# Gate and up products of a GEGLU block taken two 512-token blocks at a time, one weight load for two matmuls

## The chip, the core and the metric

The kernel runs on one core of a Trainium2 chip. Its engines run side by side and meet through semaphores: PE (TensorE, matmuls), PEld (PE's weight loads, which the profile lists apart), ACT (ScalarE), DVE (VectorE), POOL (GpSimd) and SP (which here only issues DMAs). The metric is the time of one execution on the device, in microseconds; of several runs the median is given.

## What is computed

The input `x` has 2048 tokens of 640 values, in bfloat16. Two branches are mixed by a gate per token:

```
x = A_x
g = sigmoid((x * gate_w).sum(-1, keepdims=True))
a = linear_attention(x, A_wqkv, A_wo)                       # 32 heads of 20
b = (gelu(x @ B_w_gate) * (x @ B_w_up)) @ B_w_down          # 640 -> 1728 -> 640
return g * a + (1 - g) * b
```

The change concerns `x @ B_w_gate`, `x @ B_w_up`, the gelu and the product of the two.

## The kernel before

Everything lies in one SBUF tensor, `pool`, and one PSUM tensor, `ps`, of 8 banks of 128 x 512 float32. The transposed input `xT` has 5 chunks `k` of 128 model dimensions; a matmul's weights are a 128 x 128 block, its moving operand 128 x 512 (one block `j` of 512 tokens, one bank of output).

The stages in order: the q and k products and their feature maps (L453 to L558), the product of keys and x with its evacuation (L596 to L634), then the long loop over `ffn`, which this change is in, then the output stage (L811 to L876), which adds the attention part and the down product in PSUM, scales it and sends it out.

The loop at the end of the attention setup runs over g = 0 to 55: 14 blocks `fc` of hidden units by 4 token blocks `j`, `j` the inner one. `G(g)` makes one block: five matmuls of the gate weights into one bank and five of the up weights into another (L700), a gelu of the gate bank on ACT into one of three float32 buffers `ge` (L706), and a multiply of the up bank by it on DVE into `hT` (L708). The last hidden block is only 64 wide: for `fc` = 13, `G13` has gate and up weights in the two halves of one weight block, so one bank and five matmuls a call (L678), gelu at L682, multiply at L685.

Banks come from a rotation of three pairs, which G and W2 share:

```
PAIRS = [(0, 1), (2, 3), (6, 7)]
def next_pair():
    p = PAIRS[pair_ctr[0] % 3]
    pair_ctr[0] += 1
    return p
```

In the text P0, P1 and P2 are these pairs. A G of one block takes a pair and uses its first bank for gate and its second for up. Banks 4 and 5 belong to KV; G13 takes 4, 5, 6, 7 in turn.

Other work is put between the G calls by the loop: `KV(0)` after g = 5 and `KV(1)` after g = 6 (L721, mask at L727), `W2(c)` after each of g = 8 to 13 (two short matmuls at L739 and L740 into a pair, a copy on ACT at L742, DMAs through SP), and from g = 14 on `N(i)` after each even g: a product on POOL (L754), five operations on DVE (L756 to L764) and a transpose DMA through SP. After the loop the w_down loads are issued on SP, once N has freed their place.

The order on each engine is the order of the calls of `P.op(engine, fn, reads, writes)`. It works out what each operation must wait for from its reads and writes (a bank written by PE waits for those that read it last), attaches the waits to the operation's first instruction and one semaphore increment to its last. A `P.op` of ten matmuls thus tells others of its end once. Each engine then works its list off in order.

Of the kernel before, what the change touches and what calls it, by code (L numbers as in the profile page):

```python
# [6 lines left out]
ACT = mybir.ActivationFunctionType  # L7
ALU = mybir.AluOpType
# [8 lines left out]
KC = D // 128  # L17
# [145 lines left out]
def bass_gated_mix__linear_attn_block__geglu_ffn__prompt_kernel(  # L163
# [63 lines left out]
    with (  # L227
# [8 lines left out]
        with contextlib.ExitStack() as stack:  # L236
            dma_sems = [stack.enter_context(nc.semaphore("s_in%d" % i)) for i in range(n_dma_in)]

            P = _Plan(["pe", "act", "dve", "pool", "sp"])
# [9 lines left out]
            def new_dma_key():  # L249
                k = "in%d" % dma_next[0]  # L250
                dma_next[0] += 1
                return k

            def v16(o, n):
                return pool[:, o:o + n]

            def v32(o, n):
                return pool[:, o:o + 2 * n].bitcast(F32)
# [7 lines left out]
            xT = v16(R_XT, KC * S).rearrange("p (k s) -> p k s", k=KC)  # L266
# [5 lines left out]
            wg = v16(R_WG, KC * 1664).rearrange("p (k f) -> p k f", k=KC)  # L272
            wu = v16(R_WG + KC * 1664, KC * 1664).rearrange("p (k f) -> p k f", k=KC)
            wgu = v16(R_WG + 2 * KC * 1664, KC * 128).rearrange("p (k f) -> p k f", k=KC)
# [8 lines left out]
            hT = [v16(R_B + fc * S, S) for fc in range(NFC)]  # L283
# [5 lines left out]
            ge = [v32(R_E + n * 1024, 512) for n in range(3)]  # L289
# [15 lines left out]
            bank = [P.res("bank%d" % b, excl=True) for b in range(8)]  # L305
            r_xn = [P.sb("xn%d" % i, R_XN + i * XW, R_XN + (i + 1) * XW) for i in range(NT)]
            r_pk = [P.sb("pk%d" % i, R_PK + i * 640, R_PK + (i + 1) * 640) for i in range(NT)]
            r_xT = [P.sb("xT%d" % i, R_XT, R_XT + KC * S) for i in range(NT)]
# [5 lines left out]
            r_wg = P.sb("wg", R_WG, R_WG + KC * 1664)  # L314
            r_wu = P.sb("wu", R_WG + KC * 1664, R_WG + 2 * KC * 1664)
            r_wgu = P.sb("wgu", R_WG + 2 * KC * 1664, R_WG + 2 * KC * 1664 + KC * 128)
# [20 lines left out]
            r_ratio = P.res("ratio")  # L337
            r_gw = P.res("gw")

            def dma_in(dst, src, writes, reads=(), eng="sp"):  # L340
                P.op(eng, lambda e, dst=dst, src=src: e.dma_start(dst, src),  # L341
                     reads=reads, writes=writes, dma=new_dma_key())
# [3 lines left out]
            def load_x(i, eng="sp"):  # L346
                dma_in(x_aug[:, i, 0:640], A_x[0, i * 128:(i + 1) * 128, :], [r_xn[i]], eng=eng)

            def load_wk(k, eng="sp", after=()):
                dma_in(wk[:, k, :], A_wqkv[k * 128:(k + 1) * 128, 640:1280], [r_wk[k]], reads=after, eng=eng)  # L350
# [6 lines left out]
            def load_wq(k, eng="sp"):  # L357
                dma_in(wq[:, k, 0:640], A_wqkv[k * 128:(k + 1) * 128, 0:640], [r_wq[k]], eng=eng)
# [3 lines left out]
                 writes=[P.res("touch")], dma=new_dma_key())  # L362
# [25 lines left out]
            for c in range(NHC):  # L388
# [9 lines left out]
                 reads=[r_ones], writes=[r_ident])  # L398
# [167 lines left out]
            for i in range(NQ, NT):  # L566
                KQ(i)
                if i == 4:
                    late_constants()
            P.op("dve", lambda e: e.tensor_scalar(gg, eg, 0.5, 0.5, ALU.mult, ALU.add),  # L570
                 reads=r_eg, writes=[r_g])
            P.op("dve", lambda e: e.tensor_scalar(omg, eg, -0.5, 0.5, ALU.mult, ALU.add),
                 reads=r_eg, writes=[r_omg])
# [7 lines left out]
                 reads=[r_omg], writes=[r_od], dma=new_dma_key())  # L581
# [44 lines left out]
            def ME(g):  # L626
# [6 lines left out]
                for c in cs:  # L633
# [8 lines left out]
                 reads=r_pk[0:2], writes=[r_tmp[0]])  # L642
            for i in range(2, NT):
                P.op("dve", lambda e, i=i: e.tensor_tensor(zacc, zacc, pk[i], ALU.add),  # L644
                     reads=[r_tmp[0], r_pk[i]], writes=[r_tmp[0]])
# [7 lines left out]
            r_hT = [[P.sb("hT%d_%d" % (fc, j), R_B + fc * S + j * 512, R_B + fc * S + (j + 1) * 512)  # L653
                     for j in range(NSC)] for fc in range(NFC)]
            r_ge = [P.sb("ge%d" % n, R_E + n * 1024, R_E + (n + 1) * 1024) for n in range(3)]
# [5 lines left out]
# [5 lines that stand above are left out]
            ffn = [(fc, j) for fc in range(NFC) for j in range(NSC)]  # L666
            single_ctr = [0]

            def G13(g):
                fc, j = ffn[g]  # L670
                n = g % 3
                b = (4, 5, 6, 7)[single_ctr[0] % 4]
                single_ctr[0] += 1

                def fn(e):
                    last = None
                    for k in range(KC):
                        last = e.matmul(ps[:, b, :], wgu[:, k, :], xT[:, k, j * 512:(j + 1) * 512],  # L678
                                        start=(k == 0), stop=(k == KC - 1))
                    return last  # L680
                P.op("pe", fn, reads=[r_wgu] + r_xT[4 * j:4 * j + 4], writes=[bank[b]])
                P.op("act", lambda e: e.activation(ge[n][64:128, :], ps[0:64, b, :], ACT.Gelu_apprx_tanh),  # L682
                     reads=[bank[b]], writes=[r_ge[n]])
                h = j % 2
                P.op("dve", lambda e: e.tensor_tensor(  # L685
                    hT[fc][64 * h:64 * h + 64, j * 512:(j + 1) * 512], ps[64:128, b, :], ge[n][64:128, :], ALU.mult),
                    reads=[bank[b], r_ge[n]], writes=[r_hT[fc][j]])

            def G(g):
                fc, j = ffn[g]  # L690
                if fc == 13:
                    return G13(g)
                gb, ub = next_pair()
                n = g % 3

                def mk(w, b):
                    def fn(e):
                        last = None
                        for k in range(KC):
                            last = e.matmul(ps[:, b, :], w[:, k, fc * 128:(fc + 1) * 128],  # L700
                                            xT[:, k, j * 512:(j + 1) * 512], start=(k == 0), stop=(k == KC - 1))
                        return last
                    return fn
                P.op("pe", mk(wg, gb), reads=[r_wg] + r_xT[4 * j:4 * j + 4], writes=[bank[gb]])
                P.op("pe", mk(wu, ub), reads=[r_wu] + r_xT[4 * j:4 * j + 4], writes=[bank[ub]])
                P.op("act", lambda e: e.activation(ge[n], ps[:, gb, :], ACT.Gelu_apprx_tanh),  # L706
                     reads=[bank[gb]], writes=[r_ge[n]])
                P.op("dve", lambda e: e.tensor_tensor(hT[fc][:, j * 512:(j + 1) * 512], ps[:, ub, :],  # L708
                                                      ge[n], ALU.mult),
                     reads=[bank[ub], r_ge[n]], writes=[r_hT[fc][j]])  # L710

            def KV(h):
                cs, b = (((0, 1, 2, 3), 4), ((4, 5), 5))[h]

                def fn(e):
                    last = None
                    for n, c in enumerate(cs):
                        e0 = 120 * c if c < 5 else 512
                        w = 120 if c < 5 else 40
                        for k in range(KC):  # L720
                            last = e.matmul(ps[:, b, n * 120:n * 120 + w], wv[:, k, e0:e0 + 128],  # L721
                                            mT[:, k, 120 * c:120 * c + w], start=(n == 0 and k == 0),
                                            stop=(k == KC - 1), skip_group_check=True)
                    return last
                P.op("pe", fn, reads=[r_wv] + r_mT + r_mTt, writes=[bank[b]])
                lo, hi = (0, 480) if h == 0 else (480, 640)
                P.op("dve", lambda e: e.tensor_tensor(kvl[:, lo:hi], ps[:, b, 0:hi - lo], mask[:, lo:hi],  # L727
                                                      ALU.mult),
                     reads=[bank[b], r_mask], writes=[r_kvl[h]])
# [40 lines left out]

            n_done = 0
            for g in range(len(ffn)):
                G(g)
                if g in (5, 6):
                    KV(g - 5)
                if 8 <= g < 8 + NHC:
                    W2(g - 8)
                if g == 16:
                    r_ob = P.sb("omgb", R_OB, R_OB + 2 * S)
                    dma_in(omg_b, omg_dram.unsqueeze(0).broadcast_to([128, S]), [r_ob], reads=[r_od])  # L780
                if g >= 14 and g % 2 == 0 and n_done < NT:
                    N(n_done)
                    n_done += 1
# [145 lines left out]
```

## Time and profile before

| | |
|---|---|
| median of 3 runs | 273.87 us (273.70 to 273.97) |
| the profiled execution, first to last instruction (span) | 272.6 us, granted TensorE clock 1.00 |
| median less that span | 1.27 us |
| gate and up products begin / N begins / 64-wide block begins / output stage begins | 70.4 / 106.7 / 185.9 / 190.0 us |
| last matmul starts | 270.5 us |

The profiled execution's time is known by its span alone; the times of runs come from other executions. A group line of the profile reads: line, engine, operation, output <- input, shape, count | busy time in us, mean ns of one | idle time of the engine before them, and what ended it. In an answer in order of time a line reads: start and length in us, engine, line, operation, shapes, count, and in brackets the idle time before. A line of the chain that ended last reads: start, length, engine, line, count. A few per cent of the matmul records can be missing. Busy time by stage, in us:

| from : to | PE | PEld | DVE | ACT | POOL |
|---|---|---|---|---|---|
| 70.4 : 83.4 (G to KV) | 12.95 | 5.88 | 4.74 | 5.46 | 2.77 |
| 86.9 : 103.7 (G with W2) | 16.69 | 8.19 | 5.01 | 7.69 | 0.00 |
| 103.7 : 170.8 (G with N) | 66.78 | 30.43 | 62.71 | 19.20 | 19.67 |
| 170.8 : 190.2 (G, G13) | 19.30 | 8.82 | 9.52 | 5.94 | 0.00 |
| 190.2 : 272.6 (output) | 80.17 | 36.71 | 4.13 | 11.47 | 0.00 |

### The profile page before, as it was taken

What the parts mean: (1) busy time and instruction counts of PE and PEld (TensorE: products, weight loads), DVE (VectorE), ACT (ScalarE), POOL (GpSimd) and SP (SyncE); (2) the same over time, 40 slices, a digit from 0 to 9 for tenths busy, and PEclk for the clock granted to TensorE, in tenths of its full rate; (3) what the DMA queues carried; (4) which work ended last, traced back from release to release, by engine and by line L of the source; (5) the groups of instructions that cost most, each with busy time, mean ns of one, the idle gap of its engine ahead of it and who ended that gap; (6) DMA issues with size and microseconds to landing.
All of it is one profiled execution on the core that took longest, in us unless ns stands there. A gap on an engine that the chain in (4) does not pass through costs nothing.

```text
span 272.6 us, 3416 instructions
## 1 busy us (share of the span) xinstructions
PE 267.6 (98%) x1341; PEld 127.9 (47%) x1367; DVE 140.8 (52%) x247; ACT 75.9 (28%) x132; POOL 30.0 (11%) x28
## 2 busy tenths in 40 slices
PE   8999999999999999999999999999999999999997
PEld 3555555544445454444444444444444444444444
DVE  1678989997233335999999999634210000000200
ACT  2455555210422453232222233224011122121021
POOL 5000000003240002242332422000000000000000
DMA  7976999600200011514121221273031110110211
GB/s 192 202 115 127 346 399 388 140 2 19 58 19 2 23 50 51 192 34 49 26 48 25 49 48 27 60 219 105 5 77 38 41 38 19 38 41 19 58 58 41
DMA packets 42864, 23.78 MB, mean 87 GB/s; under 512 B 32223, under 2 KB 41439, under 8 KB 42719
## 3 DMA queue, kind: packets, MB, share of 16 engines
q1 hardware_dynamic: 42517, 23.22, 31.9%
q10 hardware_dynamic: 330, 0.33, 0.3%
q8 instruction: 11, 0.18, 0.3%
q14 instruction: 6, 0.05, 0.1%
HBM read 13.83 MB, written 2.63 MB: 60 GB/s over the span
## 4 chain that ended last, share of the span: by engine, by line
PE 96%; DMA 1%; SPq 1%; issue 1%; DVE 0%
PE ps L700 41%; PE ps L864 23%; PE ps L539 12%; PE ps L596 6%; PE ps L843 4%; PE ps L468 2%; PE ps L811 2%; PE ps L678 2%; PE ps L599 1%; DMA pool<-in_A_x_dram 1%; PE ps L453 1%; PE ps L824 1%; SPq L341 1%; PE ps L721 1%; SPq L353 0%
## 5 line engine op out<-in xcount | busy, mean ns | idle before, releaser
L700 PE MATMUL ps<-pool 128*128 128x512 bf16 x510 | 113.0, 379 | 0.5
L700 PEld LDWEIGHTS ps<-pool 128*128 128x128 bf16 x520 | 50.5, 98 | 60.0
L864 PE MATMUL ps<-pool 128*128 128x512 bf16 (+2 forms) x300 | 62.4, 366 | 0.3
L706 ACT ACTIVATE pool<-ps 128x512 f32<-128x512 f32 x52 | 31.0, 597 | 73.1 <-PE ps L700 73.1
L708 DVE TENSOR_TENSOR pool<-ps,pool 128x512 bf16<-128x512 f32 x52 | 34.7, 689 | 31.7 <-PE ps L700 30.4
L864 PEld LDWEIGHTS ps<-pool 128*128 128x128 bf16 x306 | 29.2, 98 | 33.4 <-issue 0.4
L847 DVE TENSOR_TENSOR pool<-ps,pool 128x512 bf16<-128x512 f32 x4 | 2.8, 690 | 61.5 <-PE ps L843 61.5
L539 PE MATMUL ps<-pool 128*128 128x512 bf16 (+1 forms) x176 | 32.5, 343 | 0.2
L754 POOL TENSOR_TENSOR pool<-pool 128x640 f32<-128x640 bf16 x16 | 22.4, 1404 | 73.0 <-DVE pool L756 65.6
L871 ACT ACTIVATE pool<-ps,pool 128x512 bf16<-128x512 f32 (+1 forms) x16 | 10.9, 680 | 68.6 <-PE ps L864 68.6
L539 PEld LDWEIGHTS ps<-pool 128*128 128x128 bf16 x180 | 17.6, 98 | 15.0
L558 DVE SCALAR_TENSOR_TENSOR pool<-ps,pool 128x128 bf16<-128x128 f32 (+2 forms) x36 | 21.7, 602 | 2.1
L549 ACT ACTIVATE pool<-ps 128x640 bf16<-128x640 f32 x24 | 16.9, 703 | 15.8 <-DVE pool L558 9.3
L596 PE MATMUL ps<-pool 128*128 128x512 bf16 x76 | 19.2, 379 | 0.1
L764 DVE TENSOR_TENSOR pool<-pool 128x640 bf16<-128x640 bf16 x16 | 13.2, 826 | 0.6
L762 DVE TENSOR_SCALAR pool<-pool 128x32 f32<-128x32 f32 x16 | 12.8, 802 | 0.6
L756 DVE TENSOR_REDUCE pool<-pool 128x32 f32<-128x640 f32 x16 | 12.9, 808 | 0.0
L644 DVE TENSOR_TENSOR pool<-pool 128x640 f32<-128x640 f32 x14 | 11.6, 826 | 0.5
L843 PE MATMUL ps<-pool 128*128 128x512 bf16 x51 | 11.5, 379 | 0.1
L646 POOL PARTITION_ALL_REDUCE pool<-pool x1 | 4.0, 3971 | 61.0 <-DVE pool L644 61.0
L596 PEld LDWEIGHTS ps<-pool 128*128 128x128 bf16 x78 | 7.0, 98 | 7.3
L555 DVE TENSOR_SCALAR pool<-pool 128x640 bf16<-128x640 bf16 x24 | 7.9, 327 | 1.7 <-ACT pool L549 0.4
(70 smaller groups left out, 124.1 us busy)
## 6 DMA issues: line engine op xcount, KB each, us to landing
out_dram<-pool SPq DMA_DIRECT2D x19, 128.0 KB, 1.7
pool<-in_B_w_gate_dram SPq DMA_DIRECT2D x1, 2080.0 KB, 14.8
pool<-in_B_w_up_dram SPq DMA_DIRECT2D x1, 2080.0 KB, 18.0
pool<-in_A_wqkv_dram SPq DMA_DIRECT2D x8, 160.0 KB, 3.1
pool<-in_A_x_dram SPq DMA_DIRECT2D x1, 1280.0 KB, 9.2
pool<-in_A_x_dram SPq DMA_DIRECT2D x1, 1120.0 KB, 6.3
pool<-in_B_w_down_dram SPq DMA_DIRECT2D x1, 1120.0 KB, 6.4
pool<-omg_row SPq DMA_DIRECT2D x1, 1024.0 KB, 4.8
```

Of the source, the lines that this page charges most:

```text
L539: last = e.matmul(ps[:, b + p, 0:c1 - c0], xT[:, k, i * 128:(i + 1) * 128], wkq[:, k, c0:c1], start=(k == 0), stop=(k == KC - 1))
L549: P.op("act", lambda e: e.activation(e_buf[m], ps_flat[:, o:o + 640], ACT.Exp), reads=banks, writes=[r_e[m]])
L558: P.op("dve", lambda e, c0=c0, c1=c1: e.scalar_tensor_tensor(dst[:, c0:c1], ps_flat[:, o + c0:o + c1], 1.0 + EPS, e_buf[m][:, c0:c1], ALU. ...
L596: last = e.matmul(ps[:, b, :], pk[i][:, c * 128:(c + 1) * 128], x_aug[:, i, 0:512], start=(i == 0), stop=(i == NT - 1))
L700: last = e.matmul(ps[:, b, :], w[:, k, fc * 128:(fc + 1) * 128], xT[:, k, j * 512:(j + 1) * 512], start=(k == 0), stop=(k == KC - 1))
L706: P.op("act", lambda e: e.activation(ge[n], ps[:, gb, :], ACT.Gelu_apprx_tanh), reads=[bank[gb]], writes=[r_ge[n]])
L708: P.op("dve", lambda e: e.tensor_tensor(hT[fc][:, j * 512:(j + 1) * 512], ps[:, ub, :], ge[n], ALU.mult), reads=[bank[ub], r_ge[n]], write ...
L754: P.op("pool", lambda e: e.tensor_tensor(tmp[n], pq[i], z_b, ALU.mult), reads=[r_pq[i], r_zb], writes=[r_tmp[n]])
L756: P.op("dve", lambda e: e.tensor_reduce(den[n], tmp[n].rearrange("p (h d) -> p h d", h=32), AX.X, ALU.add), reads=[r_tmp[n]], writes=[r_de ...
L764: P.op("dve", lambda e: e.tensor_tensor(pq[i].rearrange("p (h d) -> p h d", h=32), pq[i].rearrange("p (h d) -> p h d", h=32), den[n].unsqu ...
L843: last = e.matmul(ps[:, b, :], wd[:, fc, 512:640], hT[fc][:, j * 512:(j + 1) * 512], start=False, stop=(fc == NFC - 2), skip_group_check=True)
L864: last = e.matmul(ps[:, pb, 0:c1 - c0], lhs, rhs, start=False, stop=(q == len(rows) - 1), skip_group_check=True)
```

## The change

A call of G now makes two token blocks, j0 and j0 + 1, and the loop calls it for even g only. For each chunk k the weight block is loaded once: the first matmul is an ordinary one, the second is made by `mm_keep`, whose instruction says that it has no weight load of its own. G takes two pairs of banks: the gate products of both blocks go into one, the up products into the other. Each of the two groups is one operation of ten matmuls. Both gelus wait for the end of the gate group, both multiplies for that of the up group. G13 takes banks 4 and 5, then 6 and 7. The calls of KV, W2 and N stand at the same g as before; two W2 calls thus follow each other, and an N follows both blocks.

```diff
+            def mm_keep(e, out_, lhs, rhs, start, stop):
+                return e.add_instruction(mybir.InstMatmult(
+                    name=nc.get_next_instruction_name(), engine=e.engine,
+                    ins=(e.lower_ap(rhs), e.lower_ap(lhs)), outs=(e.lower_ap(out_),),
+                    start_tensor_calc=start, stop_tensor_calc=stop, tile_size=(128, 128), tile_position=(0, 0),
+                    ldweights=False))
...
             def G13(g):
-                fc, j = ffn[g]
-                n = g % 3
-                b = (4, 5, 6, 7)[single_ctr[0] % 4]
+                fc, j0 = ffn[g]
+                bs = ((4, 5), (6, 7))[single_ctr[0] % 2]
...
             def G(g):
-                fc, j = ffn[g]
+                fc, j0 = ffn[g]
                 if fc == 13:
                     return G13(g)
-                gb, ub = next_pair()
-                n = g % 3
-
-                def mk(w, b):
+                gb, ub = next_pair(), next_pair()
+
+                def mk(w, bs):
                     def fn(e):
                         last = None
                         for k in range(KC):
-                            last = e.matmul(ps[:, b, :], w[:, k, fc * 128:(fc + 1) * 128],
-                                            xT[:, k, j * 512:(j + 1) * 512], start=(k == 0), stop=(k == KC - 1))
+                            for t, b in enumerate(bs):
+                                j = j0 + t
+                                args = (ps[:, b, :], w[:, k, fc * 128:(fc + 1) * 128],
+                                        xT[:, k, j * 512:(j + 1) * 512])
+                                st = dict(start=(k == 0), stop=(k == KC - 1))
+                                last = mm_keep(e, *args, **st) if t else e.matmul(*args, **st)
                         return last
                     return fn
...
+                xs = r_xT[4 * j0:4 * j0 + 8]
+                P.op("pe", mk(wg, gb), reads=[r_wg] + xs, writes=[bank[b] for b in gb])
+                P.op("pe", mk(wu, ub), reads=[r_wu] + xs, writes=[bank[b] for b in ub])
+                for t in range(2):
+                    j = j0 + t
+                    n = (g + t) % 3
+                    P.op("act", lambda e, n=n, t=t: e.activation(ge[n], ps[:, gb[t], :], ACT.Gelu_apprx_tanh),
+                         reads=[bank[gb[t]]], writes=[r_ge[n]])
+                    P.op("dve", lambda e, n=n, t=t, j=j: e.tensor_tensor(
+                        hT[fc][:, j * 512:(j + 1) * 512], ps[:, ub[t], :], ge[n], ALU.mult),
+                        reads=[bank[ub[t]], r_ge[n]], writes=[r_hT[fc][j]])
...
             for g in range(len(ffn)):
-                G(g)
+                if g % 2 == 0:
+                    G(g)
                 if g in (5, 6):
                     KV(g - 5)
                 if 8 <= g < 8 + NHC:
```

More of the change, by code (lines that the diff above doesn't have):

```diff
@@ L677, in fn @@
                     for k in range(KC):
-                        last = e.matmul(ps[:, b, :], wgu[:, k, :], xT[:, k, j * 512:(j + 1) * 512],
-                                        start=(k == 0), stop=(k == KC - 1))
-                    return last
[L681 to L687, printed above, removed]
+                        for t, b in enumerate(bs):
+                            j = j0 + t
+                            mm = mm_keep if t else e.matmul
+                            args = (ps[:, b, :], wgu[:, k, :], xT[:, k, j * 512:(j + 1) * 512])
+                            st = dict(start=(k == 0), stop=(k == KC - 1))
+                            last = mm(e, *args, **st) if t else mm(*args, **st)
+                    return last
+                P.op("pe", fn, reads=[r_wgu] + r_xT[4 * j0:4 * j0 + 8], writes=[bank[b] for b in bs])
+                for t, b in enumerate(bs):
+                    j = j0 + t
+                    n = (g + t) % 3
+                    P.op("act", lambda e, n=n, b=b: e.activation(ge[n][64:128, :], ps[0:64, b, :],
+                                                                 ACT.Gelu_apprx_tanh),
+                         reads=[bank[b]], writes=[r_ge[n]])
+                    h = j % 2
+                    P.op("dve", lambda e, n=n, b=b, h=h, j=j: e.tensor_tensor(
+                        hT[fc][64 * h:64 * h + 64, j * 512:(j + 1) * 512], ps[64:128, b, :], ge[n][64:128, :],
+                        ALU.mult), reads=[bank[b], r_ge[n]], writes=[r_hT[fc][j]])
             def G(g):
-                fc, j = ffn[g]
+                fc, j0 = ffn[g]
                 if fc == 13:
                     return G13(g)
-                gb, ub = next_pair()
-                n = g % 3
-                def mk(w, b):
+                gb, ub = next_pair(), next_pair()
+                def mk(w, bs):
                     def fn(e):
@@ L699, in fn @@
                         for k in range(KC):
-                            last = e.matmul(ps[:, b, :], w[:, k, fc * 128:(fc + 1) * 128],
-                                            xT[:, k, j * 512:(j + 1) * 512], start=(k == 0), stop=(k == KC - 1))
-                        return last
-                    return fn
[L704 to L710, printed above, removed]
+                            for t, b in enumerate(bs):
+                                j = j0 + t
+                                args = (ps[:, b, :], w[:, k, fc * 128:(fc + 1) * 128],
+                                        xT[:, k, j * 512:(j + 1) * 512])
+                                st = dict(start=(k == 0), stop=(k == KC - 1))
+                                last = mm_keep(e, *args, **st) if t else e.matmul(*args, **st)
+                        return last
+                    return fn
+                xs = r_xT[4 * j0:4 * j0 + 8]
+                P.op("pe", mk(wg, gb), reads=[r_wg] + xs, writes=[bank[b] for b in gb])
+                P.op("pe", mk(wu, ub), reads=[r_wu] + xs, writes=[bank[b] for b in ub])
+                for t in range(2):
+                    j = j0 + t
+                    n = (g + t) % 3
+                    P.op("act", lambda e, n=n, t=t: e.activation(ge[n], ps[:, gb[t], :], ACT.Gelu_apprx_tanh),
[3 more added lines that the diff above has]
+                        reads=[bank[ub[t]], r_ge[n]], writes=[r_hT[fc][j]])
             def KV(h):
```

## The prediction

> **What bounds the kernel now.** I read the page's first part, the chain that ended last, the costliest groups, then the merged instructions in order of time for PE and DVE.
>
> ```profile
> span 272.6 us, 3416 instructions
> PE 267.6 (98%) x1341; PEld 127.9 (47%) x1367; DVE 140.8 (52%) x247; ACT 75.9 (28%) x132; POOL 30.0 (11%) x28
> ```
> ```profile
> PE 96%; DMA 1%; SPq 1%; issue 1%; DVE 0%
> ```
> ```profile
> L700 PE MATMUL ps<-pool 128*128 128x512 bf16 x510 | 113.0, 379 | 0.5
> L700 PEld LDWEIGHTS ps<-pool 128*128 128x128 bf16 x520 | 50.5, 98 | 60.0
> ...
> L708 DVE TENSOR_TENSOR pool<-ps,pool 128x512 bf16<-128x512 f32 x52 | 34.7, 689 | 31.7 <-PE ps L700 30.4
> ```
>
> The chain is PE at 96%, and L700, the line that is changed, waited 0.5 us in all. So PE's own pace sets the end, and any new wait of PE goes into the time whole, unless later slack takes it back; there is none (no other engine is on the chain). The question is whether a weight load costs PE anything. A matmul's 379 ns overlaps its neighbours; its price is the step from start to start. From the chain in order of time:
>
> ```profile
> 114.27 10.74 PE ps L700 x49
> 125.06 10.74 PE ps L700 x49
> ```
>
> 49 matmuls in 10.74 us, the last one 0.379: (10.74 - 0.38) / 48 = 215.8 ns a step, each with a load of 98 ns that runs beside the matmul before it. By the records' start times the step is 55.8 ns for 128 columns (L864's cut tile), 162.5 for 384 and 215.8 for 512: a slope of (215.8 - 55.8) / 384 = 0.4167 ns a column, and 215.8 - 512 x 0.4167 = 2.5 ns that no column explains. Matmuls of 128 columns step at 55.8 ns with a 98 ns load each, so loads are no bound at four times that length.
>
> **The change part by part.**
>
> *Loads taken away.* 26 calls of G for the 128-wide blocks and 2 of G13 hold 26 x 2 x 5 + 2 x 5 = 270 pairs, so 270 of 540 loads go (520 of L700, 20 of L678). What they give PE: no matmul of this trace runs without its own load, so I bound it. At least nothing (the load is hidden wholly). At most, by the step rows, the 2.5 ns that columns don't explain: 270 x 2.5 = 0.68 us. On the other side a load could become exposed after a matmul that has none. The nearest row is the switch to 64-row matmuls at L824: from the last L811 start at 191.971 to 192.283, 0.312 us where 0.216 is usual, 0.096 us for a load that couldn't run ahead; 270 x 0.096 = 25.9 us. I take zero, nearest to the step rows: today's load starts 2 ns after the previous matmul's start and needs 98 of its 216 ns, and after the change it has the whole second matmul of a pair to do the same.
>
> The Trainium skill's "TensorE: Matmul & The Clock Gate", section "Wait — 56ns, not 53.3ns?", puts these 2.5 ns down as a fixed cost of each matmul, downstream of decode; by it the saving is zero. No row here can show that.
>
> *Banks taken in pairs of pairs.* This is the price. G now takes two of the three bank pairs, the gate products in one, the up products in the other, and PE tells of each group by one semaphore at its end. With W2 taking one pair each, the take order modulo three is: G(8) gate P2, up P0; W2(0) P1; W2(1) P2; G(10) gate P0. So G(10)'s gate needs the pair that G(8)'s up products have just filled, and between them stand only two W2 calls, as these are made for every g and G only for even g. Likewise G(12) needs G(10)'s up pair, P1, and G(14) G(12)'s, P2. Three times PE waits for two DVE multiplies that can't start before the up group ends. The rows, PE then DVE:
>
> ```profile
> 98.78 0.22 PE L740 MATMUL ps<-pool 128*120 128x128 bf16 x1
> 98.83 2.32 PE L700 MATMUL ps<-pool 128*128 128x512 bf16 x10
> 100.99 0.38 PE L739 MATMUL ps<-pool 128*120 128x512 bf16 x1
> 101.21 0.22 PE L740 MATMUL ps<-pool 128*120 128x128 bf16 x1
> 101.27 2.32 PE L700 MATMUL ps<-pool 128*128 128x512 bf16 x10
> ```
> ```profile
> 103.62 0.69 DVE L708 TENSOR_TENSOR pool<-ps,pool 128x512 bf16<-128x512 f32 x1 [1.74 <-PE ps L700]
> ...
> 118.40 1.29 DVE L708 TENSOR_TENSOR pool<-ps,pool 128x512 bf16<-128x512 f32 x2
> 119.61 0.81 DVE L756 TENSOR_REDUCE pool<-pool 128x32 f32<-128x640 f32 x1
> 120.46 0.18 DVE L759 TENSOR_SCALAR pool<-pool 128x32 f32<-128x32 f32 x1
> 120.67 0.35 DVE L761 RECIPROCAL pool<-pool 128x32 f32<-128x32 f32 x1
> 121.06 0.88 DVE L762 TENSOR_SCALAR pool<-pool 128x32 f32<-128x32 f32 x1
> 121.98 0.83 DVE L764 TENSOR_TENSOR pool<-pool 128x640 bf16<-128x640 bf16 x1
> 122.72 1.29 DVE L708 TENSOR_TENSOR pool<-ps,pool 128x512 bf16<-128x512 f32 x2
> ```
>
> Let E be the end of the up group (101.27 + 2.32 = 103.59 in the row). The multiply starts at E + 0.03 (103.62); two take 1.29, so E + 1.32. PE's load after a DVE release comes 0.05 us later (L558 ended at 49.21, the load of L611 that waited for it started at 49.27), its matmul at once: E + 1.38. Without the wait: matmuls start 0.38 - 0.22 = 0.16 before their predecessor's end, and one W2 holds PE from 100.99 to 101.27, 0.27; two make E - 0.16 + 0.54 = E + 0.38. Each wait costs 1.38 - 0.38 = 1.00 us, three 3.0. DVE idles 1.74 us before each multiply there, so nothing queues ahead. Queued behind the waiting gate group on PE are only its own up products and the next W2, and their consumers on ACT and DVE wait with it. The W2 copies go to ACT, 0.70 us each, and W2(1), W2(3) and W2(5) take gate pairs whose gelus ended before. SP's copies of w2c are later by as much, and are first read at 190.
>
> *Elsewhere the same rotation costs nothing.* Without W2 the pair of an up group is taken again two groups (4.32 us) later: PE needs it at E + 4.16, DVE frees it at E + 1.38; 2.8 us of cover. That matters from g = 14 on, where DVE is full: two multiplies and N's five operations run from 118.40 to 122.72, 4.32 us, and PE's two blocks take 20 x 215.8 = 4.32. L762's 0.88 us among them ends with POOL's L754 (0.24 us once POOL is done). Now both multiplies stand ahead of N, so DVE starts each round at E + 0.03 and ends as the next begins. Should a round be longer than PE's, DVE falls behind by the excess, and PE feels it once 15 rounds make 2.8 us, 0.19 us a round.
>
> *N one block later.* N(i) stood between the two multiplies' blocks and now follows both: 2.16 us later against PE. Its transposes go through SP ahead of the w_down loads; the last of these, issued at 178.72 and landing 8.4 us later, would land at 189.3 (plus the 3.0 that PE is late as well). O_ffn_T needs them at 193.25: 3.9 us of cover.
>
> *G13 and its end.* The last G13 fills banks 6 and 7 together. The old last block had its gelu 0.48 us after its last matmul's start, the multiply 0.62 after that. Now the second multiply starts 0.60 after the first and ends 0.48 + 0.62 + 0.60 + 0.69 = 2.39 after it, the load may go at 2.45; O_half's first load goes at 192.279 - 189.813 = 2.47 today. A tie: 0 to 0.1 us, I take 0. KV(0) stays after the same six blocks; KV(1) moves one block back, and still has a whole G before W2(0).
>
> *Sum.* 272.6 + 3.0 - 0 = 275.6 of span. What lies around the span is 273.87 - 272.6 = 1.27 us if the profiled execution is like the median: 273.87 + 3.0 = **276.9 us**, slower by 1.1%.
>
> **Rivals.**
>
> *A load exposed after a matmul without one.* Against it: the step rows. For it: no row shows the order load, matmul, matmul, load. It gives up to 276.9 + 25.9 = 302.8; at a tenth of that, 279.5.
>
> The same page, section "Step-by-step: what each phase is for", lets PE pull a load ahead of running matmuls when it goes to the background weight buffer; by it this rival falls. The rows show such a load one matmul ahead, never two.
>
> *DVE as the bound* in the N stage: DVE is at 62.7 of 67.1 us there. Rounds lengthened by 0.3 us would cost 15 x 0.3 - 2.8 = 1.7 us: 278.6.
>
> *The faster side: loads do cost PE.* If a kept matmul steps shorter by x, the three waits are paid back at x = 3.0 / 270 = 11.2 ns, beyond the 2.5 of the rows. Its far end is a whole load, 98 ns: 276.9 - 26.5 = 250.4. Against it: 512 columns at the slope of all sizes are 213.3 ns, so a step can't fall by 11 without streaming faster than any row.
>
> *The waits don't show*, as PE would meet freed banks: 273.9 less up to 0.68. Only if my take order were wrong.
>
> *The change doesn't do what it says* (loads still issued): 276.9 all the same, as I count their loss at nothing.
>
> **The numbers.** Forecast's case 0.80 (its own range 276.2 to 277.2: 0.68 saved, 0.1 for each wait's reading error); exposed load 0.07; DVE 0.06; faster 0.04; no waits 0.03. From 276.0 to 278.0 holds the forecast's case with room for a mild form of the two slower rivals. A measurement of this kernel tells about 0.2% (0.55 us) from no change. Faster 0.04, same 0.03, slower 0.93.
>
> **What would show it.** Loads of the gate and up line 260 and of G13 10, with the step still 215.8 (zero saved) or near 213.3 for half of the steps (0.68 saved). PE's waits for the DVE multiply: three of about 1.0 us, ahead of G(10), G(12) and G(14), none beyond. DVE with no idle time between two multiplies and N, and PE without waits there. Wrong if PE's step grows after a kept matmul, if waits come in every round from g = 14, or if the three waits are missing.

## The result and the profile after

The change makes the kernel slower: 276.94 us (median of 6 runs, 276.57 to 278.27) against 273.98 (median of 6, 273.70 to 275.07) for the kernel before. The ratio is 1.0114, 95% interval 1.0095 to 1.0133.

In the changed kernel the gate and up matmuls stand on two lines: L718 has those with a load, L341 those without. L729 is the multiply, L760 and L761 are W2, L886 and L865 the output tiles, L460 and L461 products of the first stage. The lines of the page that answer to those of before:

```profile
span 277.0 us, 3077 instructions
...
PE 269.4 (97%) x1341; PEld 102.3 (37%) x1097; DVE 139.6 (50%) x247; ACT 72.7 (26%) x132; POOL 29.9 (11%) x28
...
PE 96%; DVE 2%; DMA 1%; issue 1%; SPq 0%
...
L341 PE MATMUL ps<-pool 128*128 128x512 bf16 x270 | 102.3, 379 | 1.6 <-DVE pool L729 1.1
L718 PE MATMUL ps<-pool 128*128 128x512 bf16 x249 | 94.4, 379 | 1.7 <-DVE pool L729 1.7
...
L718 PEld LDWEIGHTS ps<-pool 128*128 128x128 bf16 x260 | 25.4, 98 | 87.4 <-issue 78.0
```

270 loads are gone (1367 to 1097, L718's 260 in place of L700's 520) and PEld's busy time fell from 127.9 to 102.3 us, yet no time came of it. DVE, which had 0% of the chain, now has 2%. (The busy times of L341 and L718 overlap and don't add up to PE's time.) Who waited for DVE, from the waits of the same run (engine and line, what they waited for: us in total, times, longest):

```profile
PEld ps L718 <- DVE pool L729: 3.4, 3, 1.2
...
PE ps L718 <- DVE pool L729: 1.7, 2, 0.8
...
PE ps L341 <- DVE pool L729: 1.1, 1, 1.1
```

Three times, and not once more. PE in order of time around the second of them, with DVE's three pairs of multiplies in this stretch behind it:

```profile
100.39 0.38 PE L341 MATMUL ps<-pool 128*128 128x512 bf16 x1
100.61 0.38 PE L760 MATMUL ps<-pool 128*120 128x512 bf16 x1
100.82 0.22 PE L761 MATMUL ps<-pool 128*120 128x128 bf16 x1
100.88 0.38 PE L760 MATMUL ps<-pool 128*120 128x512 bf16 x1
101.09 0.22 PE L761 MATMUL ps<-pool 128*120 128x128 bf16 x1
102.15 0.39 PE L718 MATMUL ps<-pool 128*128 128x512 bf16 x1 [0.84 <-DVE pool L729]
102.38 0.38 PE L341 MATMUL ps<-pool 128*128 128x512 bf16 x1
102.59 0.38 PE L718 MATMUL ps<-pool 128*128 128x512 bf16 x1
```
```profile
94.93 1.29 DVE L729 TENSOR_TENSOR pool<-ps,pool 128x512 bf16<-128x512 f32 x2 [3.19 <-PE ps L341]
100.81 1.29 DVE L729 TENSOR_TENSOR pool<-ps,pool 128x512 bf16<-128x512 f32 x2 [4.59 <-PE ps L341]
106.68 1.29 DVE L729 TENSOR_TENSOR pool<-ps,pool 128x512 bf16<-128x512 f32 x2 [4.59 <-PE ps L341]
```

The up group ends at 100.39 + 0.38 = 100.77, two W2 calls follow, DVE multiplies from 100.81 to 102.10, and G(12) starts at 102.15. The bracket's 0.84 is the idle time behind the modelled end of L761; what the wait costs is read from start to start: 1.060 us from the last L761 to L718, where 0.056 is usual without a wait, so 1.00. The other two are 1.00 each as well (at the first, the record of the waiting matmul is missing: 1.285 to its partner, less 0.226, the step to the partner at the other two, and 0.056).

One thing has to be known to compare the spans. The profiled execution of the changed kernel took 278.27 us, the longest of the six; the others have spans of 275.3 to 275.9. Its first matmuls ran at half pace, the last of them from 8.4 us on; in the profile of the kernel before the last slow one starts at 4.9 us. In the changed kernel:

```profile
5.16 0.63 PE L460 MATMUL ps<-pool 128*128 128x512 bf16 x1
5.58 0.31 PE L461 MATMUL ps<-pool 128*128 128x128 bf16 x1
5.69 0.63 PE L460 MATMUL ps<-pool 128*128 128x512 bf16 x1
```

A pair steps by 0.53 us here and by 0.27 (5.34 to 5.61) in the kernel before at the same point. The next stage then starts at 17.59 instead of 16.30. 277.0 - 272.6 = 4.4 us is this 1.3 and three waits of 1.0, and 0.04 at the end of G13. The code up to there is the same, so the 1.3 is no part of the change; the medians differ by 2.96.

### The profile page after: what moved, and what is told of

It is laid out like the page before. It is cut to its first block, busy times and chain, and to the rows that moved or that the text cites. A ratio compares the mean times of both kernels' runs of the same rounds, so it can differ in the third digit from the quotient of the medians.

```text
span 277.0 us, 3077 instructions
## 1 busy us (share of the span) xinstructions
PE 269.4 (97%) x1341; PEld 102.3 (37%) x1097; DVE 139.6 (50%) x247; ACT 72.7 (26%) x132; POOL 29.9 (11%) x28
## 4 chain that ended last, share of the span: by engine, by line
PE 96%; DVE 2%; DMA 1%; issue 1%; SPq 0%
PE ps L886 22%; PE ps L341 22%; PE ps L718 20%; PE ps L546 12%; PE ps L603 6%; PE ps L865 4%; PE ps L460 2%; PE ps L475 2%; PE ps L833 2%; PE ps L606 1%; DVE pool L729 1%; DMA pool<-in_A_wqkv_dram 1%; PE ps L689 1%; PE ps L846 1%; PE ps L461 1%
## 5 line engine op out<-in xcount | busy, mean ns | idle before, releaser
L341 PE MATMUL ps<-pool 128*128 128x512 bf16 x270 | 102.3, 379 | 1.6 <-DVE pool L729 1.1
L718 PE MATMUL ps<-pool 128*128 128x512 bf16 x249 | 94.4, 379 | 1.7 <-DVE pool L729 1.7
L886 PE MATMUL ps<-pool 128*128 128x512 bf16 (+2 forms) x300 | 62.2, 366 | 0.5 <-issue 0.2
L718 PEld LDWEIGHTS ps<-pool 128*128 128x128 bf16 x260 | 25.4, 98 | 87.4 <-issue 78.0
L729 DVE TENSOR_TENSOR pool<-ps,pool 128x512 bf16<-128x512 f32 x52 | 33.5, 686 | 36.7 <-PE ps L341 36.7
L727 ACT ACTIVATE pool<-ps 128x512 f32<-128x512 f32 x52 | 28.2, 595 | 79.1 <-PE ps L341 79.1
L886 PEld LDWEIGHTS ps<-pool 128*128 128x128 bf16 x306 | 29.1, 98 | 33.5 <-issue 0.4
L869 DVE TENSOR_TENSOR pool<-ps,pool 128x512 bf16<-128x512 f32 x4 | 2.8, 691 | 60.9 <-PE ps L865 58.8
L546 PEld LDWEIGHTS ps<-pool 128*128 128x128 bf16 x180 | 17.6, 98 | 15.0
L603 PE MATMUL ps<-pool 128*128 128x512 bf16 x76 | 19.2, 379 | 0.1
L865 PE MATMUL ps<-pool 128*128 128x512 bf16 x51 | 11.4, 379 | 0.0
L603 PEld LDWEIGHTS ps<-pool 128*128 128x128 bf16 x78 | 7.0, 98 | 7.3
## 6 DMA issues: line engine op xcount, KB each, us to landing
pool<-in_B_w_up_dram SPq DMA_DIRECT2D x1, 2080.0 KB, 18.4
```

The costliest lines, as they stand in the source:

```text
L341: return e.add_instruction(mybir.InstMatmult(name=nc.get_next_instruction_name(), engine=e.engine, ins=(e.lower_ap(rhs), e.lower_ap(lhs)), ...
L546: last = e.matmul(ps[:, b + p, 0:c1 - c0], xT[:, k, i * 128:(i + 1) * 128], wkq[:, k, c0:c1], start=(k == 0), stop=(k == KC - 1))
L603: last = e.matmul(ps[:, b, :], pk[i][:, c * 128:(c + 1) * 128], x_aug[:, i, 0:512], start=(i == 0), stop=(i == NT - 1))
L718: last = mm_keep(e, *args, **st) if t else e.matmul(*args, **st)
L727: P.op("act", lambda e, n=n, t=t: e.activation(ge[n], ps[:, gb[t], :], ACT.Gelu_apprx_tanh), reads=[bank[gb[t]]], writes=[r_ge[n]])
L729: P.op("dve", lambda e, n=n, t=t, j=j: e.tensor_tensor(hT[fc][:, j * 512:(j + 1) * 512], ps[:, ub[t], :], ge[n], ALU.mult), reads=[bank[ub ...
```

## Experiments

The theory on trial is that of the prediction: PE streams matmuls of 512 columns at 215.8 ns with or without a load, and the whole loss is three waits of PE for the multiplies of the G call just before. Rival 1: a load is worth up to 2.5 ns. Rival 2: part of the loss comes from matmuls without loads, or from the stage where DVE is full.

### W2 spread out: the change without its waits

```diff
-                if 8 <= g < 8 + NHC:
-                    W2(g - 8)
-                if g == 16:
+                if g % 2 == 0 and 8 <= g < 8 + 2 * NHC:
+                    W2((g - 8) // 2)
+                if g == 20:
```

> The change as it is, but one W2 after each G from g = 8 to g = 18 instead of two after each of three G (and the load of omg_b at g = 20, behind the last W2). Each G then takes P2 for gate and P0 for up, and W2 takes P1, so a gate group needs a pair freed by gelus and an up group a pair freed 2.3 us after the last up group ended, where DVE needs 1.4. My theory (the three bank waits are the whole loss, a load is worth nothing): no PE wait for L729, about 273.9 us, the time of the kernel before within 0.2%. Rival 1 (a kept matmul saves up to 2.5 ns): 273.2 to 273.9. Rival 2 (a part of the loss comes from the matmuls without loads or from waits in the stage with N): above 274.5.

Measured: 273.87 us (11 runs) against 273.85 of the kernel before (21 runs, shared by these four experiments), ratio 0.9996 (0.9985 to 1.0007). G's lines in this run:

```profile
L341 PE MATMUL ps<-pool 128*128 128x512 bf16 x270 | 102.3, 379 | 0.0
L718 PE MATMUL ps<-pool 128*128 128x512 bf16 x260 | 98.5, 379 | 0.0
```

No idle time before either. Spreading the six short W2 calls over six G calls, with nothing else of the change undone, gives back all that the change cost, and no more: rival 2 falls, and of rival 1's 0.68 us (0.25%) nothing is seen; the interval's lower end allows 0.4 us.

### All loads back, in the change and with W2 spread out

```diff
-                                last = mm_keep(e, *args, **st) if t else e.matmul(*args, **st)
+                                last = e.matmul(*args, **st)
```

> The change with an ordinary matmul in place of each one without a load, so 540 loads for the gate and up products again; banks and order as in the change. My theory: three waits of 1.0 us as before, steps of 215.8 ns, 276.9 us, the same as the change within 0.2%. Rival 1 (a load costs up to 2.5 ns): up to 277.6. Rival 2 (the matmuls without loads slow PE): faster than the change, towards 273.9 by as much as they cost.

Measured: 276.88 us (4 runs), ratio 1.0112 (1.0098 to 1.0126). The line with all its loads has the same waits:

```profile
L718 PE MATMUL ps<-pool 128*128 128x512 bf16 x520 | 113.2, 379 | 2.5 <-DVE pool L729 2.5
```

The step at the three waits is 1.058, 1.059 and 1.058 us here, 1.00 each over 0.056. The same edit in the kernel with W2 spread out:

> The spread W2 calls and all loads: two-block groups and nothing else of the change. My theory: 273.9 us, equal to w2_spread within 0.2%. Rival 1: up to 0.68 us above w2_spread. Rival 2: below w2_spread.

Measured: 273.98 us (11 runs, 273.78 to 275.98), ratio 1.0015 (1.0000 to 1.0031). Against w2_spread that is 0.11 us more, with intervals that overlap; against the change, all_loads is 0.06 us less. The two differences have opposite signs and are below what these runs can tell. The steps tell more. In the change a matmul without a load starts 215.97 ns after its partner and the next one with a load 215.68 ns after that, 215.83 on average of 492 steps; with all loads it is 215.83 (511 steps). So 270 loads are worth less than 270 x 0.01 ns, which is nothing. That the two steps of a pair differ comes from the records, whose starts are whole ns: in all_loads as in the change, five steps of 216 are followed by one of 215, 1295 ns for six or 215.83 each, and as six is even, the 215 keeps falling on the same step of a pair. In longer_dve_round, further down, it is mostly the other step (215.77 and 215.90).

### The up products block by block: is the wait made of the multiplies?

```diff
-                P.op("pe", mk(wu, ub), reads=[r_wu] + xs, writes=[bank[b] for b in ub])
+                for t in range(2):
+                    P.op("pe", up(t), reads=[r_wu] + xs, writes=[bank[ub[t]]])
```

`up(t)` is five ordinary matmuls of block j0 + t.

> The change, but the up products block by block, each block five ordinary matmuls and an operation of its own; the gate products stay in pairs with one load for two. The first multiply can then start 1.08 us before the end of the second block, so only one multiply is left behind the end E of the up products: free at E + 0.03 + 0.69 + 0.05 = E + 0.77 where PE would come at E + 0.38. My theory: three waits of 0.4 us, 273.9 + 1.2 = 275.1 us. Rival (the wait is a fixed cost of a semaphore or of W2, not the two multiplies): 276.9 as the change.

Measured: 275.14 us (5 runs), ratio 1.0045 (1.0033 to 1.0058); 275.1 was expected. DVE and PE around the first of the waits (the multiply is L739 and W2 L770 and L771 in this kernel):

```profile
92.52 0.69 DVE L739 TENSOR_TENSOR pool<-ps,pool 128x512 bf16<-128x512 f32 x1 [2.70 <-ACT pool L737]
93.60 0.69 DVE L739 TENSOR_TENSOR pool<-ps,pool 128x512 bf16<-128x512 f32 x1 [0.39 <-PE ps L728]
```
```profile
93.67 0.38 PE L770 MATMUL ps<-pool 128*120 128x512 bf16 x1
93.89 0.22 PE L771 MATMUL ps<-pool 128*120 128x128 bf16 x1
94.35 0.39 PE L718 MATMUL ps<-pool 128*128 128x512 bf16 x1 [0.24 <-DVE pool L739]
```

The first multiply now starts 1.08 us before the second, so only one is left when PE comes. From L771 to L718 it is 0.46 us in place of 0.056: a wait of 0.41, three times, 1.22 us. The wait thus shrinks by 0.59 us, which is the one multiply that was taken off its path (1.29 - 0.69 = 0.60); a fixed cost of the semaphore would have stayed.

### Matmuls of 128 columns without loads

```diff
-                        last = e.matmul(ps[:, b1, 0:128], lhs, wk[:, k, 512:640],
-                                        start=(k == 0), stop=(k == KC - 1))
+                        last = mm_keep(e, ps[:, b1, 0:128], lhs, wk[:, k, 512:640],
+                                       start=(k == 0), stop=(k == KC - 1))
```

and so in QM (129 columns) and the last product of MM; all in the kernel before.

> The kernel before, with 55 matmuls of 128 or 129 columns made without a load of their own, each behind a matmul of 512 columns with the same weights (20 of KM, 20 of QM, 15 of the last product in MM). Where a step is 55.8 ns, 2.5 ns is 4.5% of it and a load of 98 ns is longer than the matmul, so a cost of a load shows best here. My theory (a load is hidden at any of these lengths): steps of 55.8 ns as before, time within 0.2% of the kernel before. Rival 1 (a load costs 2.5 ns): steps of 53.3, 0.14 us less in all, below what a time can show but plain in the steps. Rival 2 (a load behind a matmul without one is exposed): the 512-column matmul after it starts up to 98 ns after it instead of 55.8, 55 x 42 ns = 2.3 us more, 276.2.

Measured: 274.05 us (11 runs) against 274.09 (15 runs), ratio 0.9996 (0.9987 to 1.0005). The steps behind the short matmuls are 56.0 ns (14 of MM) and 56.5 (20 of QM), where the kernel before has 55.6 and 56.8. Weight loads and matmuls of QM in this run:

```profile
11.36 0.10 PEld L475 LDWEIGHTS ps<-pool 128*128 128x128 bf16 x1 [0.17 <-DVE pool L499]
11.63 0.10 PEld L475 LDWEIGHTS ps<-pool 128*128 128x128 bf16 x1 [0.17 <-issue]
```
```profile
11.36 0.22 PE L341 MATMUL ps<-pool 128*128 128x129 bf16 x1
11.42 0.38 PE L475 MATMUL ps<-pool 128*128 128x512 bf16 x1
11.63 0.22 PE L341 MATMUL ps<-pool 128*128 128x129 bf16 x1
11.69 0.38 PE L475 MATMUL ps<-pool 128*128 128x512 bf16 x1
```

The load of the next weights starts together with the short matmul that has none (11.36), and the matmul that needs it starts 0.06 us later, although the load's record is 0.10 long. So the 98 ns of a record is not a time that a matmul waits out, and here a load is hidden even behind 56 ns. The 2.5 ns a step that columns don't explain stay without a load, so they don't come from the load. This settles rival 1 where it would have shown best, and the rival of the exposed load.

### A longer round on DVE: how much cover is there?

```diff
+                for _ in range(2):
+                    P.op("dve", lambda e: e.tensor_scalar(den[n], den[n], 1.0, None, ALU.mult),
+                         reads=[r_den[n]], writes=[r_den[n]])
```

in N, behind the operation that waits for POOL.

> The change with two more DVE operations in each N (den times 1.0, 128x32, 0.215 us from start to start each, by L759's row), placed behind the one that waits for POOL: the round of DVE in the stage with N becomes 4.316 + 0.43 = 4.75 us against 4.317 of PE. My theory (2.8 us of cover in the rotation of banks): DVE falls behind by 0.43 us a round for 15 rounds, 6.45 us, and PE feels what is over 2.8: waits from the seventh round on, 3.7 us more than the change, 280.6 us. Rival (no cover, DVE and PE locked): 6.5 us more, 283.4. Rival (PE not tied to DVE there): 276.9.

Measured: 280.16 us (4 runs) against 274.09, ratio 1.0217 (1.0203 to 1.0231). That is 3.2 us above the change's median, or 3.1 when each is taken against the kernel before in its own runs (6.07 less 2.96), not 3.7. A round of DVE late in the stage:

```profile
159.24 0.68 DVE L729 TENSOR_TENSOR pool<-ps,pool 128x512 bf16<-128x512 f32 x1
159.84 0.81 DVE L777 TENSOR_REDUCE pool<-pool 128x32 f32<-128x640 f32 x1
160.69 0.18 DVE L780 TENSOR_SCALAR pool<-pool 128x32 f32<-128x32 f32 x1
160.90 0.35 DVE L782 RECIPROCAL pool<-pool 128x32 f32<-128x32 f32 x1
161.29 0.88 DVE L783 TENSOR_SCALAR pool<-pool 128x32 f32<-128x32 f32 x1
162.21 0.40 DVE L786 TENSOR_SCALAR pool<-pool 128x32 f32<-128x32 f32 x2
162.64 0.82 DVE L788 TENSOR_TENSOR pool<-pool 128x640 bf16<-128x640 bf16 x1
163.38 1.28 DVE L729 TENSOR_TENSOR pool<-ps,pool 128x512 bf16<-128x512 f32 x2
```
```profile
159.36 0.38 PE L341 MATMUL ps<-pool 128*128 128x512 bf16 x1
159.99 0.39 PE L718 MATMUL ps<-pool 128*128 128x512 bf16 x1 [0.25 <-DVE pool L729]
```

The second multiply of the round before ends at 159.24 + 0.68 = 159.92, and PE, which would have started at 159.58, starts at 159.99. By start times PE feels nothing for the first six rounds; at 145.76 it waits 0.20 us (2.8 us of cover against a lag of 7 x 0.43 = 3.0), then 0.41 to 0.42 in each of seven rounds: 3.1 us. Cover and price a round were right. I counted one round too many: the last two N run after POOL is done, and their operation behind POOL takes 0.24 us instead of 0.88 (the kernel before shows this at 168.54), so the last round is no longer than PE's.

## Why the prediction was right

276.9 us was forecast and 276.94 measured; 2.96 us more than before, where 3.0 was worked out. That the medians meet within 0.04 us is in part luck: without the longest, the six executions still lie between 276.57 and 277.14. The waits behind the number are no luck; point by point:

- *Loads.* 270 gone, as counted. Taken at zero: shown by the steps (215.83 ns on average with and without) and by all_loads. Inside a group a load now starts 1 to 2 ns after the start of the matmul without a load that stands before it, so it has that matmul's whole step, as forecast. Neither bound was touched: nothing saved, nothing exposed. The Trainium skill's "TensorE: Matmul & The Clock Gate", section "Wait — 56ns, not 53.3ns?", has the 2.5 ns as a cost of each matmul; kept_128 agrees, with 56.0 ns at 128 columns without a load.
- *The three waits.* At G(10), G(12) and G(14), 1.00 us each, as forecast. w2_spread takes them away and with them the loss; up_by_block halves the multiplies behind the group and gets 0.41 for 0.40.
- *The rest of the rotation, and the full DVE.* No wait of PE from G(16) on. The round of DVE is 4.31 us in the changed kernel:

```profile
121.19 1.29 DVE L729 TENSOR_TENSOR pool<-ps,pool 128x512 bf16<-128x512 f32 x2
122.39 0.81 DVE L777 TENSOR_REDUCE pool<-pool 128x32 f32<-128x640 f32 x1
...
124.76 0.82 DVE L785 TENSOR_TENSOR pool<-pool 128x640 bf16<-128x640 bf16 x1
125.50 1.29 DVE L729 TENSOR_TENSOR pool<-ps,pool 128x512 bf16<-128x512 f32 x2
```

  The cover of 2.8 us, which the forecast only worked out, is what longer_dve_round found. The prediction's 15 rounds are 14, as the last two N run after POOL is done here too; no term of its sum rests on them, nor on its 3.0 / 270, which is 11.1 ns and not 11.2.
- *N one block later.* The output stage has no wait for w_down: the first L865 starts 0.309 us after the last 64-row matmul, 0.308 before.
- *The end of G13.* A tie, 0 to 0.1: the first 64-row matmul starts 0.356 us after its predecessor instead of 0.312, so 0.04 late.
- *The sum.* 275.6 of span was forecast for an execution like that of before; five of six have 275.3 to 275.9. The time around the span stayed 1.27 us (278.27 - 277.0). What the forecast didn't have is the first 10 us, where the executions shown here differ by up to 2 us whatever the kernel.

What the runs leave open is where the 2.5 ns of a step come from; of the possible sources they rule out only the load.

## What to carry to other kernels

Before a weight load is taken away, look at the step from matmul to matmul with its load: if it is what the columns need (here 0.4167 ns each, and 2.5), the load is hidden; taking it away gained nothing here, and PEld's busy share (47%, then 37%) told nothing of it. Grouping two outputs to share a load halves the number of steps in a rotation of banks; ask for each take of a bank how much PE work lies between the end of the group that filled it and the take, and whether the evacuation of the whole group (here 1.38 us) fits. Where it doesn't, spreading the short work between the groups gave all of it back here, and making the last group block by block gave back more than half.

## What the runs showed of the hardware

The start isn't the same from execution to execution: at first, matmuls of 512 columns step by 427 ns instead of 216. The last slow one starts at 4.9 us in the kernel before, at 8.4 in the changed one and at 10.1 in w2_spread_all_loads, whose profiled execution took 275.98 us against a median of 273.98. In all_loads it starts at 2.5. The stage behind starts at 16.3, 17.6, 18.4 and 16.2 us. The granted clock of these stretches is listed as 1.00 all the same, but this is no measurement: stretches without a clock record are listed so. The trace of the changed kernel has its first clock record, of 1.00, at 8.78 us, which is where its step changes; in w2_spread and up_by_block the first records stand at 6.87 and 4.92 us, and there too the matmul under way is the last slow one. The other five traces, that of the kernel before among them, hold no clock record. So it is the step that shows the pace. The Trainium skill's "TensorE: Matmul & The Clock Gate", section "What's actually happening", has a half-rate state that ends after a busy window whose place in time is not tied to the kernel's start; the doubled step and its varying end agree with that.
